# An attention and FFN kernel on one Trainium2 core: its build-time scheduler replaced by written-down tables of order, slots and engines

## The chip, the cores and the metric

The kernel runs on one NeuronCore of one Trainium2 chip. A core has five engines that each run their own stream of instructions in order: PE (TensorE, matrix multiplication), DVE (VectorE), ACT (ScalarE), POOL (GpSimd) and SP (SyncE, which here only issues DMA transfers). Matmuls write to PSUM; everything else lives in SBUF. The engines wait for each other by semaphores. The metric is the time of one execution on the device in microseconds, lower is better.

## The reference

Two parts follow each other. The first is causal attention over 4 batches, 8 heads, 768 tokens and head size 64, in which each query looks only at 6 chunks of 32 keys. Which ones is decided by an upper bound of the score, from the least and the greatest key of each chunk. The second is an FFN with a gate on the 3072 tokens.

```python
k_min, k_max = min and max of k over chunks of 32 tokens
ub = sum(maximum(q * k_min, q * k_max), axis=-1)       # 24 chunks for each query
ub = where(causal, ub, -1e9); top_chunks = argsort(ub)[..., -6:]
scores = q @ k.T / sqrt(64), masked to the top chunks and to earlier tokens
x = softmax(scores) @ v                                # 3072 tokens x 512
xn = x / sqrt(mean(x * x) + 1e-6) * rms_g
out = (silu(xn @ w_gate) * (xn @ w_val)) @ w_out       # 512 -> 1536 -> 512
```

Inputs and outputs are float32; matmuls of scores, values and FFN run in bf16, those of the upper bound in float32.

## The kernel before

**Tiling.** The tokens are cut into twelve blocks of 256 tokens: batch b, position m (0 to 2). They are handled in the order of a list at L501: (0,0), (1,0), (2,0), (3,0), (0,1), (1,1), (0,2), (2,1), (1,2), (3,1), (2,2), (3,2); "block 4" is the fifth of them, (0,1). Within a block the heads form two groups of four, 0 and 1.

**Attention of a block.** SP loads k, q and v (ACT helps for block 0). DVE transposes k and q in squares of 32 (L794) and takes the minimum and maximum of k for each chunk (L809). ACT or POOL converts them to bf16 ("half", L801 and L802). The upper bounds are float32 matmuls (`upper`, L680; L698 for the blocks with m = 0) of q, of its positive part ("relu", L888) and, for m > 0, of a copy with crossed partitions: SP copies these quarters from SBUF to SBUF by DMA ("qm", L864). DVE turns the bounds (L723), takes the greatest eight of each query (L739) and makes a mask (L745, L749, "swap" L755 or L759). Score matmuls (L922) add the mask by further small matmuls (L933); ACT exponentiates (L972); POOL clears the triangle of the diagonal (L942); value matmuls follow (L998); DVE divides by the sum (L1013, L1017).

**FFN of a block.** ACT squares and sums (L1034), POOL forms the inverse root (L1040, L1042). For blocks 0 to 3 DVE or ACT scales (L1066, L1068), PE transposes (L1078) and ACT or DVE evicts (L1087, L1091). For the later blocks DVE scales (L1052) and SP issues a transposing DMA ("across", L1058). Then come the gate and value matmuls (L1122): an FFN *piece* is eight matmuls of 256 columns, or sixteen of 128 in the half-block pieces of blocks 0 and 1. ACT takes the tanh (L1129), DVE multiplies (L1133), ACT copies the value half and POOL multiplies (L1141, L1144), or DVE does it directly (L1137). The projection (L1169) sums twelve matmuls of 512 columns, ten first and two later ("project" and "project+"); ACT or DVE evicts (L1184, L1187) and SP stores (L1191).

**Weights.** POOL issues nine loads of a third each of w_gate, w_val and w_out (`load_w` L625, `load_wo` L630), chained so that they stay in the order wg0, wv0, wg1, wv1, wg2, wv2, wo0, wo1, wo2. The first k, q and v loads of blocks 2 and 3 and the load of the norm's weights are tied to the landing of some of them (L584).

**What sets the order.** The program is not written in the order in which it runs. The code first makes a list of 1580 operations (`Plan.op`, L231): name, engine, a duration in which the engine is taken and one until the result is there, a function that emits the instructions, what it reads and writes, and which buffers of which pool it takes. Some (`flex`, L540) have two or three engines to choose from. Pools are small: four PSUM banks F for the upper bounds, transposes, values, FFN pieces and projections; two score buffers S, of which a score pass takes both; two output buffers; two to eighteen of the others (L453 to L480). `Plan.run` (L255) is a list scheduler at build time: it walks a modelled time forward, and for each engine picks, among the operations that could start, the one with the earliest due time of a table (`DUE`, L125). [...] It chooses the engine, hands out the buffer slots, and where PE would be idle before 60 us puts in filler matmuls ("warm", L1245) that write to a free bank. The emitted order is then fixed: on the chip each engine runs its stream in that order, and an operation that waits holds up everything behind it on its engine.

Of the kernel before, what the change touches and what calls it, by code (L numbers as in the profile page):

```python
# [11 lines left out]
ACT = mybir.ActivationFunctionType  # L12
# [7 lines left out]


# [15 lines left out]
class Rings:  # L37
    FETCHED = 3.3

    def __init__(self):  # L40
        self.now = 0.0
        self.queue = {}
        self.wait = []

    def _step(self, until):
        while True:
            heads = [q[0] for q in self.queue.values() if q]
            nxt = self.wait[0][0] if self.wait else None
            if not heads:
                if nxt is None or nxt > until:  # L50
                    return
                self.now = max(self.now, nxt)
            else:
                cycle = sum(d[1] for d in heads)
                end = self.now + min(d[0] for d in heads) * cycle
                stop = min(end, until, nxt if nxt is not None else end)
                if stop > self.now:
                    for d in heads:
                        d[0] -= (stop - self.now) / cycle
                    self.now = stop  # L60
                for q in self.queue.values():
                    if q and q[0][0] <= 1e-9:
                        q[0][2](self.now)
                        q.pop(0)
            while self.wait and self.wait[0][0] <= self.now + 1e-12:
                _, ring, d = self.wait.pop(0)
                ahead = sum(x[0] * x[1] for x in self.queue.get("POOL", ()))
                if ring != "POOL" and not d[3] and ahead > 0.0 and not self.queue.get(ring):
                    d[3] = True
                    self.wait.append((self.now + min(self.FETCHED, ahead), ring, d))  # L70
                    self.wait.sort(key=lambda w: w[0])
                    continue
                self.queue.setdefault(ring, []).append(d)
            if self.now >= until and not (self.wait and self.wait[0][0] <= until):
                if not any(q and q[0][0] <= 1e-9 for q in self.queue.values()):
                    return

    def add(self, t, ring, packets, cost, op):
        self._step(min(t, self.wait[0][0]) if self.wait else t)

        def landed(now, op=op):
            op.done = now + (0.9 if op.dma[2] else 1.2) + op.slack
        op.done = None
        self.wait.append((t, ring, [packets, cost, landed, False]))
        self.wait.sort(key=lambda w: w[0])
        self.guess()

    def room(self, ring, t):

        other = Rings()  # L90
        other.now = self.now
        other.queue = {r: [list(d) for d in q] for r, q in self.queue.items()}
        other.wait = [(w, r, list(d)) for w, r, d in self.wait]
        for q in list(other.queue.values()) + [[d for w, r, d in other.wait]]:
            for d in q:
                d[2] = lambda now: None

        def held():
            return sum(d[0] for d in other.queue.get(ring, ())) + sum(
                d[0] for w, r, d in other.wait if r == ring)  # L100

        while held() > 85.0:
            t = max(t, other.now) + 0.25
            other._step(t)
        return t

    def guess(self):
        other = Rings()
        other.now = self.now
        other.queue = {r: [list(d) for d in q] for r, q in self.queue.items()}  # L110
        other.wait = [(t, r, list(d)) for t, r, d in self.wait]
        other._step(1e9)


class Plan:

    SHARES = ("qx", "scale", "relu", "bd0", "bd1", "dk", "mk")
    PATIENT = {"DVE": 0.6, "ACT": 0.6}  # L120
    STICK = 25
    RESERVED = ("hh",)
    HOP = {"PE": 0.055, "ACT": 0.04, "DVE": 0.04, "POOL": 0.075, "SP": 0.06}

    DUE = (  # L125
# [129 lines left out]
    def run(self, in_order=(), fill=None):  # L255
# [4 lines left out]
        last = {}  # L260
# [1018 lines left out]
```

## Time and profile before

| | |
|---|---|
| median of 3 runs | 299.87 us (299.29 to 300.12) |
| profiled execution, from its first to its last instruction | 297.4 us |
| PE busy | 282.5 us (95%) |
| DVE, ACT, POOL busy | 217.1, 216.7, 155.6 us |
| DMA | 35.08 MB, 118 GB/s on the mean |
| mean granted TensorE clock | 0.997 |

Of the profiled execution the profile gives the span, not a time of its own as the runs have it; the median of the runs is 2.5 us above the span. In the profile's rows "L1122" is a line of the kernel; "F<-xsT,wg" says which tile is written from which; "x16" is a count of instructions. The page's chain of waits starts at the last instruction and goes back, at each step, to what released it. Matmuls are pipelined: a row's length includes the way through the array, so that the distance from one start to the next is the cost to PE.

### The profile page before, as it was taken

What the parts mean: (1) busy time and instruction counts of PE and PEld (TensorE: products, weight loads), DVE (VectorE), ACT (ScalarE), POOL (GpSimd) and SP (SyncE); (2) the same over time, 40 slices, a digit from 0 to 9 for tenths busy, and PEclk for the clock granted to TensorE, in tenths of its full rate; (3) what the DMA queues carried; (4) which work ended last, traced back from release to release, by engine and by line L of the source; (5) the groups of instructions that cost most, each with busy time, mean ns of one, the idle gap of its engine ahead of it and who ended that gap; (6) DMA issues with size and microseconds to landing.
All of it is one profiled execution on the core that took longest, in us unless ns stands there. A gap on an engine that the chain in (4) does not pass through costs nothing.

```text
span 297.4 us, 11418 instructions
## 1 busy us (share of the span) xinstructions
PE 282.5 (95%) x4672; PEld 213.4 (72%) x4672; DVE 217.1 (73%) x623; ACT 216.7 (73%) x372; POOL 155.6 (52%) x266
## 2 busy tenths in 40 slices
PE   7879999999999996999999999899999999999994
PEld 7548777657858854878767787488688778678763
DVE  6987774977998998888999999679356454456430
ACT  4897877688979876987985797677587668565331
POOL 4885858755976864475583276538044114214120
PEclk9999999999999999999999999999999999999998
DMA  7999998755676656654768576511014021011011
GB/s 188 208 204 206 255 197 163 159 130 134 141 194 154 144 136 103 149 100 110 205 135 162 108 193 150 133 40 39 0 57 55 1 82 30 2 73 35 2 71 71
DMA packets 86388, 35.08 MB, mean 118 GB/s; under 512 B 74816, under 2 KB 81728, under 8 KB 86336
## 3 DMA queue, kind: packets, MB, share of 16 engines
q1 hardware_dynamic: 80736, 29.12, 42.6%
q0 software_dynamic: 4752, 4.72, 9.4%
q8 instruction: 36, 0.59, 0.8%
q10 hardware_dynamic: 848, 0.53, 0.7%
q14 instruction: 16, 0.13, 0.2%
HBM read 28.58 MB, written 6.29 MB: 117 GB/s over the span
## 4 chain that ended last, share of the span: by engine, by line
PE 76%; DMA 9%; DVE 4%; ACT 4%; SPq 3%; POOL 1%; issue 1%; DVEq 0%; POOLq 0%; ACTq 0%
PE F L1122 39%; PE F L1169 18%; PE S L922 6%; PE F L998 6%; PE F L680 3%; SPq L528 3%; PE S L933 2%; DMA xsT<-xs 2%; DMA qraw<-in_q_dram 2%; DMA vraw<-in_v_dram 2%; DMA kraw<-in_k_dram 2%; DVE kx L809 1%; POOL hh L1144 1%; DVE m L739 1%; ACT th L1129 1%
## 5 line engine op out<-in xcount | busy, mean ns | idle before, releaser
L972 ACT ACTIVATE pt<-S 128x1024 bf16<-128x1024 f32 (+3 forms) x104 | 85.6, 857 | 19.7 <-PE S L933 18.2
L1144 POOL TENSOR_TENSOR hh<-tg,vs 128x512 bf16<-128x512 bf16 x48 | 55.7, 1164 | 42.6 <-ACT vs L1141 22.9
L1133 DVE SCALAR_TENSOR_TENSOR tg<-th,F 128x512 bf16<-128x512 bf16 x72 | 48.4, 680 | 39.3 <-ACT th L1129 33.7
L1122 PE MATMUL F<-xsT,wg 128*128 128x256 bf16 (+1 forms) x608 | 72.6, 267 | 3.7 <-DVE xnat L1017 1.7
L1122 PE MATMUL F<-xsT,wv 128*128 128x256 bf16 (+1 forms) x608 | 72.4, 267 | 0.6 <-DMA xsT<-xs 0.3
L1169 PE MATMUL F<-wo,hh 128*128 128x512 bf16 (+1 forms) x300 | 68.5, 371 | 1.8 <-POOL hh L1144 0.6
L1122 PEld LDWEIGHTS <-wg 128*128 128x128 bf16 x608 | 55.6, 98 | 13.5 <-issue 2.7
L1122 PEld LDWEIGHTS <-wv 128*128 128x128 bf16 x608 | 55.2, 98 | 9.7 <-DMA vraw<-in_v_dram 0.8
L1129 ACT ACTIVATE th<-F 128x512 bf16<-128x512 f32 x72 | 42.5, 598 | 19.7 <-PE F L1122 17.4
L942 POOL TENSOR_SCALAR_AFFINE_SELECT pt<-pt 128x512 bf16<-128x512 bf16 x48 | 32.2, 674 | 32.3 <-ACT pt L972 31.7
L1169 PEld LDWEIGHTS <-hh 128*128 128x128 bf16 x300 | 27.7, 98 | 28.4 <-issue 1.8
L1141 ACT ACTIVATE vs<-F 128x512 bf16<-128x512 f32 x48 | 28.7, 598 | 13.2 <-PE F L1122 10.1
L922 PE MATMUL S<-qb,kb 32*128 32x256 bf16 (+1 forms) x800 | 32.8, 253 | 2.3 <-ACT qb L801 2.0
L809 DVE TENSOR_REDUCE kx<-kT 128x16 f32<-128x512 f32 x48 | 30.4, 664 | 0.0
L998 PEld LDWEIGHTS <-pt 128*128 128x128 bf16 x672 | 24.8, 98 | 3.1 <-issue 0.3
L998 PE MATMUL F<-VX,pt 128*128 128x65 bf16 x672 | 26.6, 194 | 0.2 <-ACT vs L1141 0.2
L922 PEld LDWEIGHTS <-kb 32*128 32x128 bf16 x800 | 13.9, 92 | 15.0 <-issue 14.4
L933 PE MATMUL S<-mtd,chunkrow 32*128 32x128 bf16 (+2 forms) x384 | 20.5, 203 | 0.2 <-issue 0.2
L933 PE MATMUL S<-mto,chunkrow 32*128 32x128 bf16 (+2 forms) x384 | 19.9, 203 | 0.0
L1017 DVE TENSOR_TENSOR xnat<-F,rden 128x256 bf16<-128x256 f32 x48 | 19.2, 415 | 0.7
L933 PEld LDWEIGHTS <-chunkrow 32*128 32x128 bf16 x768 | 18.5, 93 | 1.2 <-issue 0.4
L1034 ACT ACTIVATE junk<-xnat 128x512 bf16<-128x512 bf16 x24 | 15.1, 631 | 5.4 <-DVE xnat L1017 5.0
(71 smaller groups left out, 337.2 us busy)
## 6 DMA issues: line engine op xcount, KB each, us to landing
vraw<-in_v_dram SPq DMA_DIRECT2D x24, 256.0 KB, 4.4
out_dram<-osb SPq DMA_DIRECT2D x23, 256.0 KB, 2.4
kraw<-in_k_dram SPq DMA_DIRECT2D x72, 64.0 KB, 2.4
qraw<-in_q_dram SPq DMA_DIRECT2D x72, 64.0 KB, 2.2
QX<-qT SPq DMA_DIRECT2D x32, 64.0 KB, 2.7
wg<-in_moe_w_gate_dram POOLq DMA_DIRECT2D x3, 512.0 KB, 12.3
wv<-in_moe_w_val_dram POOLq DMA_DIRECT2D x3, 512.0 KB, 14.3
wo<-in_moe_w_out_dram POOLq DMA_DIRECT2D x3, 512.0 KB, 23.5
```

The source lines that it names most:

```text
L809: plan.op(f"ext{n}{J}", "DVE", 0.585, 0.67, lambda n=n, op=op: VE.tensor_reduce(out=at(kx)[:, g, n], in_=at(kT).rearrange("p h (j c x) -> ...
L922: TE.matmul(s[a // 2][:, a % 2, c0:c0 + q1 - q0], kbt[r, t, ks], qbt[r, t, q0:q1], start=(t == 0), stop=(t == 1 and not mask), skip_group_ ...
L933: TE.matmul(o, chunkrow[r, BLK * kg + P * e:BLK * kg + P * (e + 1)], mv, start=False, stop=(d == 1), skip_group_check=True)
L942: GE.affine_select(out=d, in_=d, compare_op=ALU.is_ge, fill=0.0, base=0, pattern=[[0, 4], [1, P]], channel_multiplier=-1)
L972: lambda pt=pt, hs=hs, c0=c0, c1=c1, x=sc[hp]: SE.activation(out=at(pt)[:, hs, c0:c1], in_=at(x)[:, :, c0:c1], func=ACT.Exp, scale=SCALE), ...
L998: TE.matmul(o[:, a, :], p_[:, a, off:off + P], vt[:, e, a, :], start=(kb_ == 0 and a == 0), stop=(kb_ == nkb - 1 and a == 3), skip_group_c ...
L1122: TE.matmul(at(p_)[:, n * W:(n + 1) * W], w[:, g, ht * P:(ht + 1) * P], at(xT)[:, g, x0:x0 + W], start=(g == 0), stop=(g == NP - 1), skip_ ...
L1129: plan.op(f"tanh{U}.{hp}", "ACT", 0.48, 0.6, lambda th=th, gp=gp: SE.activation(out=at(th), in_=at(gp), func=ACT.Tanh, scale=0.5), pri - 0 ...
L1133: VE.scalar_tensor_tensor(out=at(tg), in0=at(th), scalar=1.0, in1=at(gp), op0=ALU.add, op1=ALU.mult), pri - 30, reads=[th, gp], writes=[tg ...
L1141: plan.op(f"vcopy{U}.{hp}", "ACT", 0.48, 0.6, lambda vs=vs, vp=vp: SE.activation(out=at(vs), in_=at(vp), func=ACT.Copy), pri + 0.1, reads= ...
L1144: plan.op(f"hh{U}.{hp}", "POOL", 1.11, 1.16, lambda tg=tg, vs=vs, hh=hh: GE.tensor_tensor(out=at(hh), in0=at(tg), in1=at(vs), op=ALU.mult) ...
L1169: TE.matmul(at(op)[:, cs], at(key)[:, o:o + P], wo[:, ht, cs], start=(ht == 0), stop=(ht == NHT - 1), skip_group_check=True)
```

## The change

The scheduler (`Rings`, `DUE`, the search in `Plan.run`) is removed. Four tables take its place: `SEQUENCE`, the numbers of all 1580 operations in one order, from which each engine's own order follows; `SLOTS`, the slot of each of the 1032 buffers; `CHOICE`, a letter (A, D or G for ACT, DVE or POOL) for each of the 206 operations with several engines; and `WARM`, nine places for filler with their counts. `run` only walks through the tables and asserts that an operation stands behind what it needs and that its slot is free. Some duration figures in the operations are edited too (the first blocks' conversions from 0.54 to 1.0, the mask row from 0.8 to 2.2, the weight loads' rate); nothing reads them any more. What each operation emits is unchanged.

```diff
-class Rings:
...
-    DUE = (
...
+SEQUENCE = [
+    22, 34, 37, 13, 33, 3, 35, 36, 14, 6, 38, 41, 18, 19, 4, 31, 24, 17, 29, 0, 7, 26, 39, 40, 1, 44, 48, 55,
...
+    1574, 1571, 1575, 1577, 1578, 1579]
+SLOTS = [
...
+CHOICE = (
+    "GGGGAADGGAGAAGAADDDDAGGGGADDGAGDGGAADADDGDGDGAGDDGGDGGDGDAAGGDGGAGGDGDGDGGADAGGAAGGGGGDAGGADGGGDGGGG"
+    "AAGGDGGADGDGGAAGGGGGGGGGGGAGGAGGGGDAAGGAGGGGGGAGAAGDDGGGGGGAGGGDGAGGGDAGGGGAGGAGAAAAAAAAADAAADAADDAA"
+    "ADDADA")
+WARM = [
+    (58, 86, 0, 0), (72, 4, 2, 1), (97, 10, 0, 1), (140, 6, 2, 1), (166, 2, 3, 1), (174, 5, 2, 1), (183, 1, 1,
+    1), (267, 1, 3, 1), (339, 1, 0, 1)]
...
-    def run(self, in_order=(), fill=None):
+    def run(self, fill):
+        keys = list(self.pool_of)
         left = {k: len(v) for k, v in self.readers.items()}
+        self.slot = dict(zip(keys, SLOTS))
...
+        engine = dict(zip((o.seq for o in self.ops if len(o.alts) > 1), CHOICE))
...
+        for place, x in enumerate(SEQUENCE):
+            for n, slot, wide in warm.get(place, ()):
...
+            o = self.ops[x]
+            assert all(d.seq in gone for d in o.deps + o.after) and x not in gone
+            if x in engine:
+                o.eng = self.NAMES[engine[x]]
+            o.occ, o.lat, o.fn = o.alts[o.eng]
             for key in o.takes:
...
+                place_ = (self.pool_of[key], self.slot[key])
+                assert held[place_] is None, (o.name, place_, held[place_])
+                held[place_] = key
```

The numbers say little by themselves, so here is what the tables hold, read against the list of operations. PE keeps 315 operations, and on the mean one stands 2.9 places from where it stood. ACT has 314 (before 330), DVE 436 (426), POOL 253 (247), SP 262 (262). A change of matmul shape from one PE operation to the next occurs 116 times (121). Filler is 86 narrow and 30 wide matmuls (77 and 39).

PE's order from the first FFN piece to block 1's first piece ("wg0(0) h0" is the gate piece of block 0's first half, "wg0 h6" that of the whole block from hidden tile 6; s, v, t are score pass, values, transpose with block and head group or half; "fill n" is n wide fillers):

```
before: wg0(0) h0, s1.1a, wv0(0) h0, t0.1, s1.0b, fill 2, wg0(1) h0, wg0 h4, s1.1b, wg0 h6, wv0(1) h0, wv0 h6,
        v1.0, v1.1, v1.0, v1.1, wv0 h4, fill 6, wg0 h8, wg0 h10, t1.0, fill 3, t1.1, wg1(0) h0
after:  wg0(0) h0, wv0(0) h0, fill 2, v1.0, s1.1a, fill 5, t0.1, s1.0b, fill 1, wg0 h6, v1.1, wg0(1) h0, wv0 h4,
        wv0(1) h0, s1.1b, wg0 h4, v1.0, wv0 h6, wg0 h10, v1.1, t1.0, wg0 h8, wg1(0) h0
```

The first loads on SP, and the weight loads' places on POOL (among its 253 or 247 operations):

```
SP before: k0 k0 q0 q0 v0 v0 k1 k1 k1 k1 q1 q1 q1 q1 v1 v1        POOL before: wg0 35, wv0 36, wg1 38, wv1 40, wg2 41, wv2 42, wo0 44, wo1 53, wo2 54
SP after:  k0 k0 q0 q0 k1 q1 k1 q1 q1 k1 q1 k1 v0 v0 v1 v1        POOL after:  wg0 34, wv0 42, wg1 46, wv1 49, wg2 55, wv2 56, wo0 59, wo1 61, wo2 75
```

POOL's constants (the memsets of "ones", BO and BD), all done before block 0's work in the old order, are partly spread between that work in the new one: before wg0 there now stand a conversion of block 0's k, block 0's two positive parts and four products for the bounds, and of block 1 one positive part and one q conversion.

More of the change, by code (lines that the diff above doesn't have):

```diff
@@ L34, in __init__ @@
         self.alts = {eng: (occ, lat, fn)}
-class Rings:
[L38 to L112, printed above, removed]
@@ L115 @@
-class Plan:
[L119 to L123, printed above, removed]
-    DUE = (
[91 rows of a table removed]
-    )
+class Plan:
+    NAMES = {"P": "PE", "A": "ACT", "D": "DVE", "G": "POOL", "S": "SP"}
     def __init__(self):
@@ L392, in run @@
             for key in o.uses:
-                last[key] = max(last.get(key, 0.0), o.done)
                 left[key] -= 1
                 if not left[key]:
-                    self.free[self.pool_of[key]].append((last[key], slot[key]))
+                    held[self.pool_of[key], self.slot[key]] = None
+            gone.add(x)
             order.append(o)
-            for u in o.users:
-                n_dep[u.seq] -= 1
-                if not n_dep[u.seq]:
-                    offer(u)
         self.order = order
-        self.span = max(o.done for o in order)
@@ L565, in constants @@
             -378, reads=["ident"], writes=["pat"])
-        plan.op("chunkrow", "DVE", 0.8, 0.9, lambda: VE.tensor_scalar(
+        plan.op("chunkrow", "DVE", 2.2, 2.28, lambda: VE.tensor_scalar(
             out=chunkrow.rearrange("p (c t) -> p c t", t=CH),
@@ L1245, in keep_busy @@
             TE.matmul(store["F"][slot][:, 0:x.shape[1]], ident[:], x, start=True, stop=True)
-    for o in plan.run(in_order=("kraw", "qraw", "vraw", "kT", "qT", "kb", "qb", "QX", "VX", "xsT", "xs", "hh", "xnat"),
-                      fill=(1.6, 5.6, 60.0, 0.0565, 0.216, "F", keep_busy)):
+    for o in plan.run(("F", keep_busy)):
         o.fn()
```

169 lines of the change are left out of this document (27 added, 142 removed), and 197 rows, old and new, of tables (DUE, SEQUENCE, SLOTS).

## The prediction

> **What bounds the kernel now.** I read the head of the page and its chain of waits first, then the engines' busy time in stretches, cut at the first FFN matmul (22.8 us) and at the last long wait of the start (38.6 us).
>
> ```profile
> span 297.4 us, 11418 instructions
> ...
> PE 76%; DMA 9%; DVE 4%; ACT 4%; SPq 3%; POOL 1%; issue 1%; DVEq 0%; POOLq 0%; ACTq 0%
> ...
> core 0: us, PE busy (x) PEld busy (x) DVE busy (x) ACT busy (x) POOL busy (x), PEclk, DMA share, GB/s
> 0.00:22.80 22.80, 18.35 (x349) 13.33 (x349) 18.30 (x55) 17.46 (x33) 16.84 (x60) 1.00 1.03 200
> 22.80:38.60 15.80, 14.71 (x238) 11.70 (x234) 12.07 (x33) 13.52 (x32) 11.57 (x20) 1.00 1.19 228
> 38.60:60.00 21.40, 21.31 (x324) 16.37 (x326) 15.18 (x46) 15.13 (x28) 15.00 (x25) 1.00 0.89 171
> 60.00:100.00 40.00, 38.77 (x636) 28.96 (x636) 35.39 (x120) 35.36 (x67) 27.08 (x40) 1.00 0.62 152
> 100.00:140.00 40.00, 36.67 (x723) 28.34 (x721) 34.57 (x112) 31.57 (x53) 25.14 (x37) 1.00 0.57 121
> 140.00:180.00 40.00, 40.00 (x759) 30.20 (x761) 38.23 (x115) 33.05 (x54) 20.49 (x37) 1.00 0.70 158
> 180.00:220.00 40.00, 39.13 (x718) 28.86 (x707) 27.20 (x85) 27.68 (x44) 18.53 (x28) 1.00 0.27 68
> 220.00:260.00 40.00, 40.00 (x667) 30.31 (x666) 20.23 (x37) 28.77 (x43) 13.19 (x16) 1.00 0.16 35
> 260.00:297.40 37.40, 33.56 (x291) 25.38 (x289) 15.89 (x27) 14.17 (x26) 7.76 (x8) 0.98 0.15 50
> ```
>
> PE is the bound: its work is 76% of the chain, and from 38.6 us on it is hardly ever empty. An order can only win what PE loses. Length less PE busy is 4.45 us before 22.8, 1.09 up to 38.6, 0.09 up to 60, then 1.23, 3.33, 0, 0.87, 0 and 3.84. The last 3.84 is nearly all the end (last matmuls, eviction, store), whose order stays almost as it was. Beside idle time there is filler, matmuls that only keep PE running, all before 38 us:
>
> ```profile
> L1245 PE MATMUL F<-chunkrow,ident 128*128 128x512 bf16 x39 | 10.2, 380 | 0.0
> L1245 PE MATMUL F<-ident 128*128 128x128 bf16 x77 | 6.4, 265 | 1.7 <-POOL eps L551 1.7
> ```
>
> The DMA engines are full there (share 1.03 and 1.19), so the start is paced by what arrives, and by how fast DVE and ACT turn it into the first FFN operand.
>
> **The change part by part.** Every operation is still issued once; only order, slots and engine choices differ. The durations edited in the code fed the planner that is deleted, and cost nothing on the chip.
>
> *Start, to the first FFN piece.* SP now issues block 1's k and q ahead of block 0's v. DVE does block 1's q transposes and min/max ahead of block 0's first normalisations. The first scale and the first transposed eviction go from ACT to DVE.
>
> ```profile
> 7.27 1.31 DVE L794 STREAM_TRANSPOSE qT<-qraw 128x512 f32<-128x512 f32 x2 [0.33 <-DMA qraw<-in_q_dram]
> 8.49 1.83 DVE L809 TENSOR_REDUCE kx<-kT 128x16 f32<-128x512 f32 x3
> 15.44 0.42 DVE L1017 TENSOR_TENSOR xnat<-F,rden 128x256 bf16<-128x256 f32 x1
> ...
> 19.19 0.73 ACT L1068 ACTIVATE xs<-xnat,ri_all 128x512 bf16<-128x512 bf16 x1
> 21.06 1.15 ACT L1087 ACTIVATE xsT<-F,rmsg 128x128 bf16<-128x128 bf16 x4
> ...
> 22.85 1.07 PE L1122 MATMUL F<-xsT,wg 128*128 128x128 bf16 x16
> 38.65 1.05 PE L1122 MATMUL F<-xsT,wg 128*128 128x128 bf16 x16 [0.73 <-ACT xsT L1087]
> ...
> L1091 DVE TENSOR_TENSOR xsT<-F,rmsg 128x512 bf16<-128x512 bf16 x2 | 1.4, 692 | 0.3 <-PE F L1078 0.2
> L1066 DVE TENSOR_SCALAR xs<-xnat,ri_all 128x512 bf16<-128x512 bf16 x2 | 0.7, 350 | 0.1
> ```
>
> Ahead of the normalisation that ended at 15.86 us DVE now has two more transposes (0.65 each) and four more reduces (0.61 each), 3.7 us. DVE is idle for 4.50 of the first 22.8 us (22.80 less 18.30), 1.69 of that before its first instruction, so up to 2.8 us can go into gaps. The normalisation ends between 15.86 + 0.9 = 16.8 and 15.86 + 3.7 = 19.6; I take 17.9, nearer the packed end, since q of block 1 no longer arrives behind v. From it to the first FFN matmul took 22.85 - 15.86 = 7.0 us. On DVE the scale is 0.38 shorter (0.73 to 0.35) and the eviction 0.46 (1.15 to 0.69), and both leave the ACT queue, where the scale began 3.3 us after the normalisation's end and the eviction 1.1 us after the scale. I estimate 3.9 us for what is left (square, mean, scale, transpose, eviction, with their hops). First FFN piece: 21.8, between 20.7 and 23.5.
>
> *First FFN piece to 38.65.* I laid the two PE orders side by side from the tables. Between the first piece and block 1's first piece both hold the same ten FFN pieces, three score passes and four value products; the new one has 8 instead of 11 wide fillers and one transpose less. A wide filler is 0.216 us (the chain row of 512-wide matmuls below, 2.16 for 10), a transpose of four about as much. So 15.80 becomes 14.9 with its 1.09 us of idle kept, 13.8 without; 14.35 is the middle. Block 1's first piece comes at 21.8 + 14.35 = 36.15, 2.5 earlier; the moved transpose gives 0.1 back. **Start: -2.4**, between -4.0 and +0.6.
>
> *Weights behind it.* POOL used to issue all weight loads early; now each stands behind named work. The first stands behind block 1's q conversion, the last, a third of w_out, behind a product of block 0's FFN.
>
> ```profile
> 9.80 0.99 POOL L528 DMA_DIRECT2D wg<-in_moe_w_gate_dram  x1
> 20.90 1.61 POOL L528 DMA_DIRECT2D wo<-in_moe_w_out_dram  x2
> ...
> 41.30 1.16 POOL L1144 TENSOR_TENSOR hh<-tg,vs 128x512 bf16<-128x512 bf16 x1 [0.53 <-ACT vs L1141]
> ...
> DMA to landing us min/median/max: 22.6/23.5/25.2
> DMA to landing us min/median/max: 7.9/17.8/25.2
> ...
> 49.72 2.16 PE F L1169 x10
> ```
>
> The first landing row is of the w_out loads alone, the second of all nine weight loads. The early issue bought queueing: a w_out load took 22.6 to 25.2 us, the last one, issued about 21.7, landing near 47. The bytes ahead of it are the same in both orders, so with full engines it should land as before; the first projection, which needs all of w_out, started at 49.7. It can therefore move up by the 2.4 us of the start, to just about the landing. I cost the move at nothing; without that cover each microsecond of lateness is one of PE.
>
> *Waits after 38.6 us.* The largest lie in one place:
>
> ```profile
> 105.37 3.54 SPq L528 DMA_DIRECT2D qraw<-in_q_dram  x6
> 108.96 1.87 SPq L864 DMA_DIRECT2D QX<-qT  x3
> 112.08 2.62 SPq L1058 DMA_TRANSPOSE xsT<-xs  x2
> ...
> 107.14 2.42 DVE L809 TENSOR_REDUCE kx<-kT 128x16 f32<-128x512 f32 x4
> ...
> 110.84 1.04 PE L1169 MATMUL F<-wo,hh 128*128 128x512 bf16 x4
> 111.81 0.94 PE L680 MATMUL F<-QX,BD 64*32 64x128 f32 x16
> 113.20 0.48 PE L680 MATMUL F<-qraw,BD 64*32 64x128 f32 x10 [0.44 <-POOL qraw L888]
> 117.58 1.05 PE L1122 MATMUL F<-xsT,wg 128*128 128x256 bf16 x8 [1.72 <-DVE xnat L1017]
> ```
>
> The upper bounds (L680) wait for copies that SP issues behind q loads at 0.6 us each. In the new table the last copy is 6 places earlier on SP (about 3.5 us), and PE reaches the bounds only 0.86 us sooner (four projection matmuls later instead of earlier): the 0.44 goes. The FFN of block 4 waits 1.72 us for transposed rows. Their chain loses two of the four reduces ahead of the scale (1.2 us), gains one gate product (estimated at a reduce's 0.6) and is 3 places earlier on SP; cover on PE is the same ten operations. I take half, 0.86. Of the other 3.27 us between 60 and 220 (5.43 less 2.16), whose places are all re-ordered, a third: 1.1. In block 5 one FFN piece and one score pass less stand ahead of the same wait (estimated from the 0.9 us of a projection's four matmuls as some 1.6 us less cover), against two operations that leave the DVE path ahead of the scale (about 1.2, as two reduces): +0.4, taken as +0.5. **Waits: -1.9**, between -5.4 (all gone) and +4.
>
> *Switches.* Going between full, row-tiled and quadrant matmuls leaves 0.97 - 4 x 0.216 = 0.11 us (110.84 to 111.81). The tables have 116 such changes on PE, before 121: **-0.5**.
>
> *Engine choices.* ACT has 314 operations in the tables, before 330; POOL 253, before 247; DVE 436, before 426.
>
> ```profile
> L802 POOL CAST qb<-qT 128x512 bf16<-128x512 f32 x16 | 10.6, 659 | 4.5 <-PE S L922 2.6 <-DVE qT L794 1.4 <-DVE rden L1013 0.5
> ```
>
> At such a conversion's length that is some 10 us off ACT, and, as small operations leave POOL for larger ones, an estimated 14 onto it. POOL's busy column adds up to 155.6 of 297.4, and DVE has idle time everywhere but in 140 to 180 us (1.77): hidden, and a rival if not.
>
> Sum: -2.4 - 1.9 - 0.5 = -4.8. The profiled span is 297.4, the median of the runs 299.87, 2.5 above, which start and end around the span add. 299.87 - 4.8 = **295.1 us**.
>
> [...] The shorter filler leaves PE gaps in the first 21.8 us: filler falls from 28 wide and 77 narrow to 20 and 86, and I expect up to 2 us of idle in one piece.
>
> ```profile
> 4.00:6.00 2.00, 2.00 (x24) 2.00 (x22) 1.46 (x4) 0.37 (x2) 0.29 (x2) 1.00 0.87 253
> 6.00:8.00 2.00, 2.00 (x38) 1.92 (x35) 1.67 (x4) 1.91 (x2) 0.00 (x0) 1.00 1.16 221
> ```
>
> In the filler alone PE did 24 matmuls in 2 us at first, then 38: it starts at about 0.6 of its later rate, whatever the clock column says. [...]
>
> **The rivals.**
> 1. *Nearly all PE waits go* and the start reaches its early bound: -4.0 - 4.8 - 0.5, 290.6. For it: every engine has idle time beside PE. Against: four banks and two score buffers still tie PE to ACT and DVE. 0.19.
> 2. *The weights come late* (the slower side): w_out's last load is issued behind a product of block 0's FFN that ran at 41.3 us. With the shortest landing of the rows (7.9) it lands at 49, with the shortest of a w_out load (22.6) at 64. At 54, 13 us after its issue, the first projection starts 4.3 late and the start's gain is gone: 299.87 + 4.3 - 1.9 - 0.5 = 301.8. It decides at a landing of 52.1, where lateness eats the other two gains. For it: the load stands at place 75 on POOL, before at 54. Against: with full DMA engines the bytes, not the issue, set the landing. 0.15.
> 3. *DVE absorbs it*: at 38.23 of 40 busy in 140 to 180 us it can't follow a PE that is 3 us ahead, and the waits come back there: only the switches remain, 299.4. Against: DVE has 16.3 us idle between 38.6 and 140 (6.22 + 4.61 + 5.43) that it could use. 0.06.
> 4. *The clock falls in the start*: 4 us of FFN pieces at 24/38 of the rate cost 1.5: 296.6. 0.03.
> 5. *The start gives nothing*, since arrivals pace it: 299.87 - 2.4 = 297.5. 0.10.
>
> **How the numbers follow.** My forecast has 0.47; alone it spans 292.5 to 297.0. 0.3%, 0.9 us, is about what runs of this kernel (299.29 to 300.12) can tell from no change. Faster: 0.47 + 0.19 + 0.10 + 0.03 = 0.79; same 0.05 and slower 0.16 from rivals 2 and 3 (0.01 of rival 3 falls on the slower side). The range runs from 289.5, just below rival 1, to 301.0, which leaves out the worse half of rival 2.
>
> **What the new profile would show.** Right: the first FFN matmul at 20.7 to 23.5 us, block 1's first piece near 36; first projection near 47, with no wait for w_out; L680 without the 0.44 us wait; about 9 us of PE idle beside start and end filler cut to 30 wide ones; ACT about 10 us less busy, POOL about 14 more. Wrong: PE waiting on a weight load or on POOL before 55 us, or DVE at its limit with PE idle between 140 and 180 us.

## The result, and the profile after

The tables made the kernel slower: 307.76 us, median of 4 runs (307.13 to 309.81), against 299.90 (299.29 to 300.12) for the kernel before on the same chip. The ratio is 1.0254, 95% interval 1.0203 to 1.0305. The forecast was 295.1, its range ended at 301.0. (Here and below, ratios and intervals leave out runs more than 1.5% above the fastest of the same kernel, four of eleven in the run with the wait for scale10 alone and at most two elsewhere; medians and spreads are of all runs.) The profiled execution of the new kernel took 307.62 us, 305.9 of them from its first to its last instruction.

The head of its page, the busy times and the chain that ended last:

```profile
span 305.9 us, 11386 instructions
...
PE 285.5 (93%) x4672; PEld 217.5 (71%) x4672; DVE 226.8 (74%) x633; ACT 204.3 (67%) x353; POOL 162.5 (53%) x272
...
PE 52%; DVE 18%; DMA 12%; SPq 6%; POOL 4%; issue 4%; ACT 2%; ACTq 0%; DVEq 0%; POOLq 0%
```

PE's share of the chain fell from 76% to 52%, DVE's rose from 4% to 18%. Of the 8.5 us that the span grew (305.9 less 297.4), PE is idle for 5.5 (20.4 against 14.9, span less busy) and busy for 3.0 longer (285.5 against 282.5) although nine wide fillers became narrow ones. The stretches of the prediction's table (columns as there) say where:

```profile
0.00:22.80 22.80, 18.86 (x373) 14.93 (x374) 16.69 (x57) 14.07 (x26) 15.62 (x57) 1.00 0.95 205
22.80:38.60 15.80, 13.30 (x204) 10.45 (x202) 13.34 (x29) 11.11 (x27) 11.85 (x17) 0.93 1.12 214
38.60:60.00 21.40, 18.71 (x276) 15.05 (x274) 19.50 (x41) 12.37 (x21) 14.49 (x20) 0.89 0.82 159
...
100.00:140.00 40.00, 36.53 (x770) 28.74 (x769) 35.02 (x124) 31.99 (x53) 28.27 (x42) 1.00 0.64 134
...
180.00:220.00 40.00, 36.90 (x711) 28.75 (x710) 30.56 (x95) 27.84 (x44) 18.60 (x27) 0.96 0.34 77
```

PE idle went from 1.09 to 2.50 us in the second stretch, from 0.09 to 2.69 in the third and from 0.87 to 3.10 in 180 to 220; in 100 to 140 it is 3.47, before 3.33. In the same three stretches, and only there, the granted clock (the column after POOL) is below its value of before, which made PE's own work longer (in two profiles further down the same six fillers take 2.67 us at 0.50 and 1.47 at 1.00). PE's order of time shows one long wait in each place:

```profile
34.61 1.05 PE L949 MATMUL F<-xsT,wg 128*128 128x256 bf16 x8 [1.78 <-DMA wg<-in_moe_w_gate_dram]
...
53.69 1.54 PE L949 MATMUL F<-xsT,wv 128*128 128x128 bf16 x13 [2.44 <-DVE tg L960]
...
189.88 1.17 PE L825 MATMUL F<-VX,pt 128*128 128x65 bf16 x20 [3.02 <-DVE tg L960]
```

and finer windows of PE alone (busy, count, granted clock, DMA share, GB/s), two for each gap, show the clock behind it:

```profile
33.04:36.45 3.41, 1.15 (x12) 1.00 1.22 226
36.45:39.86 3.41, 3.41 (x30) 0.50 1.24 207
50.11:53.52 3.41, 1.15 (x13) 1.00 1.22 214
53.52:56.93 3.41, 3.24 (x51) 0.50 0.61 120
186.64:190.05 3.41, 0.40 (x9) 1.00 0.39 61
190.05:193.46 3.41, 3.41 (x55) 0.50 0.61 133
```

Each time the granted clock is 0.50 for 3.41 us, which costs up to 1.7 us of full-rate work (an estimate: half of 3.41), 5.1 us for the three. Not every such gap has this behind it, as the last section shows.

What does DVE do ahead of its late tg (DVE's product with the tanh, which frees PE's bank)? In order of time, around 33 us and 48 us, first DVE, then POOL, whose hh is the product of gate and value half and whose pt is the triangle of the diagonal (each row begins with its start and its length):

```profile
32.88 3.00 DVE L893 TENSOR_SCALAR xs<-xnat,ri_all 128x512 bf16<-128x512 bf16 x1
...
48.37 4.67 DVE L572 TENSOR_TENSOR mk<-ubn,m 128x64 bf16<-128x64 f32 x1
52.96 0.67 DVE L960 SCALAR_TENSOR_TENSOR tg<-th,F 128x512 bf16<-128x512 bf16 x1
...
32.84 0.65 POOL L769 TENSOR_SCALAR_AFFINE_SELECT pt<-pt 128x512 bf16<-128x512 bf16 x1
33.45 2.27 POOL L971 TENSOR_TENSOR hh<-tg,vs 128x512 bf16<-128x512 bf16 x2
...
47.85 3.38 POOL L971 TENSOR_TENSOR hh<-tg,vs 128x512 bf16<-128x512 bf16 x3
51.18 0.63 POOL L769 TENSOR_SCALAR_AFFINE_SELECT pt<-pt 128x512 bf16<-128x512 bf16 x1
51.78 0.60 POOL L731 CAST VX<-vraw 128x512 bf16<-128x512 f32 x1
52.34 0.62 POOL L769 TENSOR_SCALAR_AFFINE_SELECT pt<-pt 128x512 bf16<-128x512 bf16 x1
```

The scale of block 1's first half ("scale10") took 3.00 us, against 0.35 for the same shape before; the mask of block (2,0), head group 1 ("mk(2,0,1)") took 4.67, where before no mask of any of the three shapes took longer than 0.99:

```profile
L745 DVE TENSOR_TENSOR mk<-ubn,m x15: 204/651/987, 12.2 to 206.7; 128x512 bf16<-128x512 f32 x8, 128x64 bf16<-128x64 f32 x6, 128x128 bf16<-128x128 f32 x1
```

Both began while POOL worked without a break and ended when POOL had nothing to do: at 35.88 behind the hh that ended at 35.72, at 53.04 behind the triangle that ended at 52.96. The planner that the change removes had a rule against just this (in its modelled time it never let an operation of a list of names, "scale" and "mk" among them, start on DVE while a POOL operation of over 0.15 us ran); tables hold an order, not a distance in time.

One operation outside that list had shown the same in the profile before: the row of chunk masks, written at the start, took 2.28 us beside POOL's memsets, and 0.55 in the changed kernel, where those memsets are spread:

```profile
2.17 2.28 DVE L566 TENSOR_SCALAR chunkrow<-pat 128x768 bf16<-128x768 bf16 x1
```

The third place is another kind. DVE's order of time there:

```profile
183.13 0.74 DVE L879 SCALAR_TENSOR_TENSOR xs<-xnat,ri_all,gB 128x512 bf16<-128x512 bf16 x1
186.96 1.24 DVE L715 TENSOR_SCALAR qraw<-QX 128x512 f32<-128x512 f32 x1 [3.09 <-DMA QX<-qT]
188.12 0.99 DVE L466 TENSOR_REDUCE BD<-kx 128x64 f32<-128x64 f32 x5
189.14 0.69 DVE L960 SCALAR_TENSOR_TENSOR tg<-th,F 128x512 bf16<-128x512 bf16 x1
```

The relu of block (2,2), group 0, is on DVE now and waits 3.09 us for SP's copies; the tg behind it, whose tanh was done at 185.19, frees the PSUM bank for PE's value product and comes at 189.14.

### The profile page after: what moved, and what is told of

The parts are those of the page before. It is cut to its first block, busy times and chain, and to the rows that moved or that the text cites. A ratio compares the mean times of both kernels' runs of the same rounds, so it can differ in the third digit from the quotient of the medians.

```text
span 305.9 us, 11386 instructions
## 1 busy us (share of the span) xinstructions
PE 285.5 (93%) x4672; PEld 217.5 (71%) x4672; DVE 226.8 (74%) x633; ACT 204.3 (67%) x353; POOL 162.5 (53%) x272
## 4 chain that ended last, share of the span: by engine, by line
PE 52%; DVE 18%; DMA 12%; SPq 6%; POOL 4%; issue 4%; ACT 2%; ACTq 0%; DVEq 0%; POOLq 0%
PE F L949 25%; PE F L996 14%; PE S L749 5%; PE F L825 5%; SPq L354 4%; DMA kraw<-in_k_dram 4%; DVE kx L636 3%; DMA QX<-qT 2%; DMA wg<-in_moe_w_gate_dram 2%; DMA qraw<-in_q_dram 2%; DVE kT L621 2%; PE S L760 2%; DVE tg L960 2%; DVE xs L879 2%; DVE m L566 2%
## 5 line engine op out<-in xcount | busy, mean ns | idle before, releaser
L949 PE MATMUL F<-xsT,wg 128*128 128x256 bf16 (+1 forms) x608 | 73.4, 270 | 3.4 <-DMA wg<-in_moe_w_gate_dram 1.8
L949 PE MATMUL F<-xsT,wv 128*128 128x256 bf16 (+1 forms) x608 | 73.6, 270 | 2.5 <-DVE tg L960 2.4
L960 DVE SCALAR_TENSOR_TENSOR tg<-th,F 128x512 bf16<-128x512 bf16 x72 | 48.5, 678 | 27.8 <-ACT th L956 24.3
L949 PEld LDWEIGHTS <-wv 128*128 128x128 bf16 x608 | 56.3, 99 | 11.6 <-issue 2.8
L769 POOL TENSOR_SCALAR_AFFINE_SELECT pt<-pt 128x512 bf16<-128x512 bf16 x48 | 31.3, 658 | 28.8 <-ACT pt L799 28.6
L825 PE MATMUL F<-VX,pt 128*128 128x65 bf16 x672 | 28.8, 195 | 7.2 <-DVE tg L960 3.0
L825 PEld LDWEIGHTS <-pt 128*128 128x128 bf16 x672 | 26.7, 99 | 11.1 <-issue 6.7
L749 PE MATMUL S<-qb,kb 32*128 32x256 bf16 (+1 forms) x800 | 33.6, 258 | 0.1
L964 DVE TENSOR_TENSOR hh<-tg,F 128x512 bf16<-128x512 bf16 x24 | 16.2, 677 | 12.6 <-PE F L949 12.1
L844 DVE TENSOR_TENSOR xnat<-F,rden 128x256 bf16<-128x256 f32 x48 | 19.9, 419 | 1.0
```

The costliest lines, as they stand in the source:

```text
L749: TE.matmul(s[a // 2][:, a % 2, c0:c0 + q1 - q0], kbt[r, t, ks], qbt[r, t, q0:q1], start=(t == 0), stop=(t == 1 and not mask), skip_group_ ...
L769: GE.affine_select(out=d, in_=d, compare_op=ALU.is_ge, fill=0.0, base=0, pattern=[[0, 4], [1, P]], channel_multiplier=-1)
L825: TE.matmul(o[:, a, :], p_[:, a, off:off + P], vt[:, e, a, :], start=(kb_ == 0 and a == 0), stop=(kb_ == nkb - 1 and a == 3), skip_group_c ...
L949: TE.matmul(at(p_)[:, n * W:(n + 1) * W], w[:, g, ht * P:(ht + 1) * P], at(xT)[:, g, x0:x0 + W], start=(g == 0), stop=(g == NP - 1), skip_ ...
L960: VE.scalar_tensor_tensor(out=at(tg), in0=at(th), scalar=1.0, in1=at(gp), op0=ALU.add, op1=ALU.mult), pri - 30, reads=[th, gp], writes=[tg ...
```

## The experiments

My theory after the comparison: two DVE operations stand still beside a busy POOL (A1, at 33 and 48 us), one DVE operation waits for a copy at the head of its queue (A2, at 184 us), and the clock falls behind each gap. The main rival: the weights come late (wg2 landed at 34.56, before 32.08; wo2 at 54.48, before 47.00), and the DVE stalls hide in their shadow. All variants are the changed kernel with two small lists applied to its tables:

```diff
+MOVES = []    # (operation, the operation that it is put ahead of in SEQUENCE)
+HOLDS = []    # (operation, an operation that it waits for)
...
+        for n, y in MOVES:
+            todo.remove(seq[n])
+            todo.insert(todo.index(seq[y]), seq[n])
...
+        if o.name in holds:
+            tc.add_manual_dep(o.inst.ins, named[holds[o.name]].inst.ins.name, ...)
```

so that their line numbers are 13 higher (L893 is L906, L572 is L585, L960 is L973), and 17 higher in the run with the choices undone.

### Two waits on POOL

```diff
-HOLDS = []
+HOLDS = [('hh(0, (1,)).0', 'scale10'), ('hh(1, (0, 1)).4', 'mk(2, 0, 1)')]
```

> Two waits are added on POOL and nothing else is changed: hh of block 0's piece (1,) 0 waits for scale10, and hh of block 1's piece 4 waits for mk(2,0,1), so that each of these two DVE operations finds POOL idle once. Theory A (a DVE operation stands still while POOL works without a break): scale10 falls from 3.00 to under 1 us, mk(2,0,1) from 4.67 to under 1 us, the 2.44 us idle of PE before the value projection of block 1's second token half goes, and the time is 302.5 to 305. Rival B (the late weights hold the kernel there): the two operations may become short, but PE then stands as long for wg2 (landed 34.56) and wo2 (landed 54.48), and the time is 306.5 to 308.5. Rival C (the two operations are long for another reason): they stay at 3.0 and 4.7 us, and the time is 307 to 310.

Ratio to before 1.0052 (1.0020 to 1.0084), median 302.1: about 6.0 us of the 7.6 came back (ratios times 300), a little more than theory A expected. The two DVE operations, and POOL's wait behind the second:

```profile
34.21 1.14 DVE L906 TENSOR_SCALAR xs<-xnat,ri_all 128x512 bf16<-128x512 bf16 x1
...
48.41 0.75 DVE L585 TENSOR_TENSOR mk<-ubn,m 128x64 bf16<-128x64 f32 x1
...
49.30 2.27 POOL L984 TENSOR_TENSOR hh<-tg,vs 128x512 bf16<-128x512 bf16 x2 [0.24 <-DVE mk L585]
```

One wait of 0.24 us on POOL turned 4.67 us on DVE into 0.75: the mask ended at 49.16, right behind the one POOL operation that ran when it began (a product, 47.89 to 49.06). PE's 2.44 us wait is gone. Rival C is out: the two operations are long because of POOL. The scale fell to 1.14, a little above "under 1". Each wait was then tried alone.

```diff
-HOLDS = []
+HOLDS = [('hh(1, (0, 1)).4', 'mk(2, 0, 1)')]
```

> The changed kernel with one added wait: hh of block 1's piece 4 waits for mk(2,0,1). Theory (the stall at 48 us is worth what PE lost there, +4.2 us between 20 and 30 us of its work): 303 to 305. Rival (PE reaches wo2's landing at 54.5 first, so that only 2 to 3 of it come back): 305 to 306.

```diff
-HOLDS = []
+HOLDS = [('hh(0, (1,)).0', 'scale10')]
```

> The changed kernel with the other wait alone: hh of block 0's piece (1,) 0 waits for scale10. Theory (worth 1 to 2 us by itself, since wg2's landing at 34.6 is right ahead of it): 305.5 to 307. Rival (the slack behind it takes it up, nothing comes back): 307 to 308.5.

With the wait for mk alone the ratio is 1.0111 (1.0065 to 1.0157), median 303.7: inside the theory's 303 to 305. The scale still took 3.36 us there, at 33.51. With the wait for scale10 alone it is 1.0081 (1.0042 to 1.0120), better than either expectation, and with the widest spread (300.6 to 308.1); its profile still has the mask at full length:

```profile
47.94 4.69 DVE L585 TENSOR_TENSOR mk<-ubn,m 128x64 bf16<-128x64 f32 x1
```

By the ratios the two alone are worth 4.3 and 5.2 us, by the medians 4.1 and 3.5, and both together 6.0 or 5.6: the prices don't add. The clock may have a part in this: in the last profile PE still waits 2.45 us behind the mask, up to 53.28, and the clock stays at 1.00 there. In the same profile the relu near 184 us also cost PE 1.3 us instead of 3.0, with nothing changed there, so a part of its gain is a later wait that came out shorter.

### One DVE operation moved

```diff
-MOVES = []
+MOVES = [('relu(2, 2, 0)', 'turn k(3, 2, 0)')]    # behind KX(2,2) and tg of piece 8
```

> One DVE operation is moved: relu(2,2,0) goes behind KX(2,2) and tg of block 6's piece 8, so that DVE no longer waits 3.09 us at it for the QX copies while both are ready. Theory A: the 3.02 us idle of PE before values(1,2,0)0 and the low clock behind it go, and the time is 303.5 to 305.5. Rival B (PE has slack there, because the copies, vx(3,1,1) or project6.1 hold it at once): 306.5 to 308.5.

Ratio 1.0181 (1.0149 to 1.0212), median 305.4: 2.2 us back, at the upper edge of what I expected, because the next wait stood behind:

```profile
187.54 1.09 DVE L728 TENSOR_SCALAR qraw<-QX 128x512 f32<-128x512 f32 x1 [0.58 <-DMA QX<-qT]
...
190.20 0.69 DVE L973 SCALAR_TENSOR_TENSOR tg<-th,F 128x512 bf16<-128x512 bf16 x1
...
190.94 1.24 PE L1009 MATMUL F<-wo,hh 128*128 128x512 bf16 x5 [1.60 <-DVE tg L973]
```

The relu still waits and still runs beside POOL (1.09 us; the relu that began in a gap of POOL at 85.61 in the changed kernel's profile took 0.41), and now the projection waits 1.60 us for the tg behind it.

### Both

```diff
-MOVES = []
-HOLDS = []
+MOVES = [('relu(2, 2, 0)', 'turn k(3, 2, 0)')]
+HOLDS = [('hh(0, (1,)).0', 'scale10'), ('hh(1, (0, 1)).4', 'mk(2, 0, 1)')]
```

> The two added POOL waits and the moved relu together. Theory A: the gains are at different times and add up, 298 to 301.5, that is, the time of the kernel before again. Rival: the later gain is taken back by what the earlier one triggers, 303 to 306.

Ratio 0.9999 (0.9967 to 1.0031), median 300.8: the time of the kernel before, as the theory had it. Two waits and one move take back the whole loss, and no more. In its profile (span 296.6) the relu takes its 0.42:

```profile
180.83 0.42 DVE L728 TENSOR_SCALAR qraw<-QX 128x512 f32<-128x512 f32 x1
```

### The rival: weights earlier

```diff
-MOVES = []
+MOVES = [('wg2', 'tri(1, 0, 0)a'), ('wv2', 'tri(1, 0, 0)a'), ('wo0', 'tri(1, 0, 1)a'),
+         ('wo1', 'hh(0, (0,)).0'), ('wo2', 'hh(0, (0,)).0')]
```

> The last five weight transfers are issued earlier, in gaps of POOL of the changed kernel: wg2 and wv2 at about 22 instead of 26.1 and 26.9, wo0 at about 25, wo1 and wo2 at about 26 and 27 instead of 32.0 and 47.0. Theory A: what stood behind the late weights is the DVE operations, so wg2's 1.78 us idle is taken over by scale10 and nothing changes at mk(2,0,1): 306 to 308.5. Rival B (the late weights hold the kernel): 302.5 to 305.

Ratio 1.0145 (1.0077 to 1.0214), median 305.3: 3.3 us back, between the two expectations. But the profile has the two DVE operations short without any added wait, and block 2's keys late:

```profile
34.63 0.71 DVE L634 STREAM_TRANSPOSE kT<-kraw 128x512 f32<-128x512 f32 x1 [2.11 <-DMA kraw<-in_k_dram]
...
37.26 0.69 DVE L906 TENSOR_SCALAR xs<-xnat,ri_all 128x512 bf16<-128x512 bf16 x1
...
50.20 0.75 DVE L585 TENSOR_TENSOR mk<-ubn,m 128x64 bf16<-128x64 f32 x1
```

The loads shifted everything in time, and both operations came out short (0.69 and 0.75 us) without the waits. So this run doesn't price the weights. A run further down, which moves only wg2 and wv2, does it in a kernel without the stalls.

### The engine choices without the order, and the order without the choices

```diff
-        engine = dict(zip((o.seq for o in self.ops if len(o.alts) > 1), CHOICE))
+        engine = dict(zip((o.seq for o in self.ops if len(o.alts) > 1), BEFORE))   # 85 letters differ
```

> The changed kernel's order, buffer slots and PE fills, but all 85 operations that the change put on another engine are back on the engine that they had before (each at its new place in the order). Theory A (the choices cost, because they put work on DVE and POOL that then stands in each other's way, and on DVE behind a copy): scale10 on ACT and relu(2,2,0) on POOL take away two of the three stalls, 301 to 305. Rival (the choices are free, as the prediction had it, and the order alone costs): 306 to 309.

Ratio 1.0282 (1.0248 to 1.0317), median 309.3: my theory that the choices cost was wrong here, the rival's 306 to 309 (just exceeded) was right. With scale10 back on ACT, DVE stands still at two other operations, one of which has only 16 elements in each partition:

```profile
37.32 2.95 DVE L659 TENSOR_TENSOR kx<-kx 128x16 f32<-128x16 f32 x1
...
50.22 2.96 DVE L589 TENSOR_TENSOR mk<-ubn,m 128x64 bf16<-128x64 f32 x1
```

So it is not one certain operation that loses the time: with other engines chosen, other DVE operations stood for 2.95 and 2.96 us near the same places.

```diff
-SEQUENCE = [22, 34, 37, ...]
+SEQUENCE = [24, 12, 34, ...]    # the order, slots and fills of the kernel before; CHOICE stays the new one
```

> The other half: the order, slots and fills of the kernel before, written as tables, with the changed kernel's 85 engine choices. Theory A (the choices cost by themselves): 302 to 307, with at least one DVE operation of over 2 us. Rival (free choices): 299.5 to 301.

Ratio 1.0153 (1.0112 to 1.0195), median 304.9. The time is what the theory had, the mechanism is not: no DVE operation took 2 us or more but the mask row at the start (2.29, before 2.28). Instead an operation that moves to another engine moves into another queue, and small waits sum up all along, as in these two stretches, in which PE idles 2.72 and 1.22 us (before 1.23 and 0):

```profile
60.00:100.00 40.00, 37.28 (x573) 27.20 (x571) 35.01 (x108) 28.94 (x56) 28.91 (x43) 1.00 0.58 141
...
140.00:180.00 40.00, 38.78 (x717) 29.25 (x715) 36.65 (x116) 29.59 (x50) 20.91 (x36) 1.00 0.66 160
```

So neither half is free and neither half is the cause by itself; order and choices fit each other, and each is bad with the other's partner.

### Is the predicted gain behind the stalls?

The kernel with both mended is as fast as before, not 4.8 us faster. A first candidate was the clock in the start. PE's window from 19 to 21 us (clock after the count) in the changed kernel, then in the kernel with both mended:

```profile
19.00:21.00 2.00, 1.78 (x18) 1.00 1.25 205
```
```profile
19.00:21.00 2.00, 2.00 (x13) 0.50 1.22 200
```

Of the eight profiles that have the changed kernel's start and fills with its engine choices, two show 1.00 there and six 0.50. At 0.50 the six fillers ahead of the first FFN transpose take 2.67 us instead of 1.47, and the first FFN piece comes at 23.03 instead of 21.55; in the kernel before it came at 22.85.

```profile
19.09 2.67 PE L1085 MATMUL F<-chunkrow,ident 128*128 128x512 bf16 x6
```

```diff
-        for at, n, slot, wide in WARM:
+        for at, n, slot, wide in WARM + [(103, 3, 3, 1), (124, 5, 3, 1)]:
```

> The kernel with both added POOL waits and the moved relu, and with eight more filling matrix multiplications on PE, three before values(0,0,1)0 and five before values(0,0,0)1, where PE waits 1.0 and 1.4 us at 14 to 17 us. Theory: the granted clock stood at 0.50 from 19 to 21 in that kernel (1.00 in the changed one's profile), which stretched the six filling multiplications before the first turn from 1.3 to 2.5 us; with the fills the clock stays at 1.00 and the time falls by 1 to 2, to 298 to 300. Rival (the clock there hangs on something else, or the start is not on the path): 300 to 302.

Ratio 1.0036 (1.0005 to 1.0067), median 301.3: nothing gained. The clock did hold, 1.00 in all these windows, and the first FFN piece came at 22.41 instead of 23.03; but the five fillers stood behind a wait for the norm whose bank they wrote to, and held the values up themselves, from 17.28 to 18.30:

```profile
17.23 1.24 PE L1085 MATMUL F<-chunkrow,ident 128*128 128x512 bf16 x5 [0.95 <-DVE xnat L857]
18.30 0.42 PE L838 MATMUL F<-VX,pt 128*128 128x65 bf16 x8
```

So with more fill the clock stood at 1.00 in this profile, but the time did not fall with it.

```diff
-MOVES = [('relu(2, 2, 0)', 'turn k(3, 2, 0)')]
+MOVES = [('relu(2, 2, 0)', 'turn k(3, 2, 0)'), ('across40', 'store1.1'), ('load q1231', 'store1.1'),
+         ('across41', 'store2.1'), ('tri(1, 1, 1)0', 'dk(2, 1, 1)')]
```

> The same with four places of the order changed: the two transposes of block 4 are issued ahead of a load of queries and two stores on SP (they are ready at 108.9 and 109.9 and go out at 110.8 and 112.3, wg of block 4 waits 1.7 us for them), and tri(1,1,1)0 goes ahead of a POOL operation, half q and relu that wait for a copy (values(1,1,1)1 waits 1.6 us for it). Theory (waits of an order can be taken out one at a time once nothing triggers a new one): 2 to 3 less than without the moves, 295 to 298. Rival (the next wait takes their place): 298 to 300.

Ratio 1.0018 (0.9987 to 1.0050), median 300.8. The rival was nearer. The moves did win at their own place (PE's waits of 1.21 and 1.69 us near 117 and 123 became 1.05 and less than 0.2), but block 5 now waits 1.50 us at 133, and the same relu waited again for copies, ran beside POOL, and PE's wait behind it grew from 1.60 to 2.50:

```profile
182.81 1.22 DVE L728 TENSOR_SCALAR qraw<-QX 128x512 f32<-128x512 f32 x1 [1.35 <-DMA QX<-qT]
```
```profile
186.33 2.32 PE L1009 MATMUL F<-wo,hh 128*128 128x512 bf16 x10 [2.50 <-DVE tg L973]
```

```diff
-MOVES = [('relu(2, 2, 0)', 'turn k(3, 2, 0)'), ...
+MOVES = [('relu(2, 2, 0)', 'turn k(3, 2, 1)'), ...
-        for at, n, slot, wide in WARM + [(103, 3, 3, 1), (124, 5, 3, 1)]:
+        for at, n, slot, wide in WARM + [(103, 3, 3, 1), (109, 3, 3, 1)]:
```

> The kernel with four places changed, and relu(2,2,0) moved once more on DVE, behind the swap, tg and hh of block 6's piece 10 instead of ahead of them; the five filling multiplications before values(0,0,0)1, which waited for a norm, are replaced by three before values(0,0,0)0. Theory A (DVE's order around relu is what costs 2.7 us there: relu waits for the QX copies till 182.7, takes 1.22 us while POOL works, and tg of piece 10, whose F bank project6.1 needs, ends only at 186.3): project6.1 starts right behind scores(1,2,1)0 and the time is 296.5 to 299. Rival (the copies or POOL's hh hold project6.1 all the same): 299.5 to 301.5.

Ratio 1.0027 (1.0001 to 1.0053), median 301.8: the rival's time or just above it. The projection's 2.50 us wait is gone, as expected, but 50 us earlier block 5's wait for its transposing DMA grew from 1.50 to 2.13:

```profile
135.17 1.03 PE L962 MATMUL F<-xsT,wg 128*128 128x256 bf16 x8 [2.13 <-DMA xsT<-xs]
```

```diff
-MOVES = [...]
+MOVES = [..., ('wg2', 'tri(1, 0, 0)a'), ('wv2', 'tri(1, 0, 0)a')]
```

> The same, with wg2 and wv2 issued at about 22 instead of 26. Theory A (the late weights cost little): the wait of 1.0 to 1.5 us for wg2 near 35 goes and the next wait, for values(1,0,1)1 or block 1's xsT, takes 0.5 to 1 of it back; 0.3 to 1 less than without. Rival B (weights had been the bound of the start): 2 or more less. Rival C (the earlier transfers take DMA time from the loads of queries and keys): the same or up to 1 more.

Ratio 1.0099 (1.0062 to 1.0136), median 303.2, 2.2 us more than without (0.0072 of 300): the sign is rival C's, the size larger than it gave. PE's wait for wg2 (0.84 us) is gone, and a longer one has taken its place, since block 2's keys take 5.0 to 6.9 us to land, without the move 3.0 to 3.2, and block 1's norm stands behind them on DVE. DVE, then PE:

```profile
35.15 0.71 DVE L634 STREAM_TRANSPOSE kT<-kraw 128x512 f32<-128x512 f32 x1 [3.28 <-DMA kraw<-in_k_dram]
```
```profile
38.56 0.42 PE L838 MATMUL F<-VX,pt 128*128 128x65 bf16 x8 [2.96 <-DVE xnat L857]
```

This answers the rival for w_gate and w_val: earlier loads cost more than they bring. Earlier w_out loads were not tried in a kernel without the stalls.

The last one keeps SP's order and the fills of the changed kernel, and mends a third stall:

```diff
-MOVES = []
-HOLDS = []
+MOVES = [('relu(2, 2, 0)', 'turn k(3, 2, 1)'), ('tri(1, 1, 1)0', 'dk(2, 1, 1)')]
+HOLDS = [('hh(0, (1,)).0', 'scale10'), ('hh(1, (0, 1)).4', 'mk(2, 0, 1)'), ('hh(2, (0, 1)).8', 'scale31')]
```

> The changed kernel with three added POOL waits (for scale10, mk(2,0,1) and scale31), relu(2,2,0) behind the hh of block 6's piece 10, and tri(1,1,1)0 ahead of the POOL operations that wait for copies; no fills, and SP's order as in the changed kernel. Theory (each mended wait keeps its worth when no transfer is moved with it): 297 to 299, faster than both kernels. Rival (the kernel's other waits take it back): 299.5 to 301.5.

Ratio 0.9994 (0.9962 to 1.0026), median 300.5. The rival was right: the same time as before. PE is busy for 282.4 us of 297.5 there, before 282.5 of 297.4. None of these versions beats the kernel before.

## Why the prediction was wrong, step by step

**Start (-2.4): right at its first point, lost at its second.** The first FFN piece came at 21.55 (21.8 predicted), by the way that the sum took: the normalisation ended at 17.74 (17.9), and 3.8 us followed (3.9). Block 1's first piece came at 38.83 instead of 36.15: where I had put 14.35 us there were 17.28, with scale10 standing for 3.00 us, 1.78 us for wg2 and 3.41 us at half clock. And the first point itself holds only where the clock does, in two of eight profiles; in the others the piece came at 23.03 to 24.37. The term was worth nothing (38.83 against 38.65 before).

**Weights ("I cost the move at nothing").** "The bytes ahead of it are the same in both orders, so with full engines it should land as before" was false: wo2 landed at 54.48 instead of 47.00, wg2 2.5 us later. For w_out it cost nothing that shows, as PE reached its first projection only at 57.71. For wg2 it cost a 1.78 us wait, which the sum lacked; yet issuing it earlier made the kernel slower. Rival 2 (0.15) had the right side and nearly the right landing (it decided at 52.1), but not the cause: in the kernel with both mended the projections began at 51.98, with no wait for w_out, whose last third landed at about 52.1, again later than in the kernel before.

**Waits after 38.6 us (-1.9, between -5.4 and +4): the step that failed.** PE's idle time from 38.6 to 220 us grew by 4.6 us (2.69 + 0.80 + 3.47 + 0.06 + 3.10 = 10.12 against 5.52), and the half clock behind the gaps took more. The single waits that I followed through the queues came out in the right direction: the 0.44 us of L680 are gone, block 4's 1.72 became 1.3. What was wrong was the rest of the sum, "a third" of the waits whose places are re-ordered taken as a gain, from before's waits alone. A new order makes new waits where there were none, and the wait behind the mask was in 38.6 to 60, a stage that had 0.09 us to lose. Nor was the gain hidden behind the stalls: with both mended, PE's idle time from 38.6 to 220 us is 5.68 us (0.33 + 0.88 + 4.05 + 0.06 + 0.36), 0.2 more than before, where the sum had 1.9 less.

**The planner removed ("cost nothing on the chip").** The durations do cost nothing. But in its modelled time the planner had kept operations such as scale10 and the mask from starting beside a working POOL, and I never asked what happens when nothing does. That is the missing term: the two added waits alone give 6.0 us back.

**Engine choices (hidden, 0).** ACT is 12.4 us less busy (10 predicted), POOL 6.9 more (14 predicted); DVE, to which I gave ten operations more and no price, is 9.7 more busy, of which the two stalls are about 7. Not hidden: in the old order the choices cost 1.5%; in the new order their undoing brought nothing (1.0282 against 1.0254). Rival 3 placed DVE's limit in 140 to 180 us; there PE idled 0.06 us.

**Switches (-0.5).** Nothing in the profiles shows it apart from the rest.

**The clock (rival 4, 0.03).** My forecast had the clock hold across gaps of up to 2 us. It was at 0.50 for 3.41 us behind one of 1.78 with one of 0.69 behind it, behind 2.44 and behind 3.02, and in six of eight starts, where no gap since the first matmul was above 1.25. Rival 4 thus came about in most profiles of the start. Its price of 1.5 us was too low by its own working (pieces of 4 us at 24/38 of the rate take 6.3, 2.3 more); the first piece came 1.5 later at half clock (23.03 against 21.55), for six fillers and not for FFN pieces.

## What to carry to other kernels

A search that orders instructions by traced durations keeps the order and loses the distance in time on which it relied: where an operation of one engine stands still beside the work of another, as scale10 (3.00 us) and the mask (4.67) did here, keeping the two apart has to become an order on the chip (one wait of POOL for a DVE operation cost 0.24 us and saved 3.9 on DVE). Before costing a re-ordering, ask of each rule that the old order was made under what keeps it on the chip once the planner is gone; a row far above its usual length, such as the 2.28 us of the mask row, shows where to ask. And on a queue in order, put an operation that waits for a DMA behind what is ready, or its wait becomes that of everything behind it (the relu's 3.09 us on DVE were followed by 3.02 on PE).

## What the runs showed of the hardware

**DVE beside POOL.** In the changed kernel's profile a small DVE operation stood still not for one POOL operation but for several that followed without a gap: mk(2,0,1) for 4.67 us across six (three products, two triangles, a conversion), scale10 for 3.00 across three. These ended when POOL was idle, 0.08 and 0.16 us behind its last operation. It isn't always so: in the run with the moved relu, the relu (187.54, 1.09 us) was through at 188.63, in the middle of two products of POOL that followed each other directly:

```profile
187.20 2.46 POOL L984 TENSOR_TENSOR hh<-tg,vs 128x512 bf16<-128x512 bf16 x2
```

What lets one operation through between two of POOL and not another was not found. The operations named here that took over 2 us (scale10, masks, kx and the mask row) were TENSOR_SCALARs and TENSOR_TENSORs with their inputs in SBUF; the SCALAR_TENSOR_TENSOR tg, with one input in PSUM, took 0.69 us beside a working POOL (from 49.62 in the run with the two waits, beside products from 49.30 to 51.57). The longest of the POOL operations that mk(2,0,1) stood across took about 1.2 us, so its 4.67 were not a wait for one of them.

**The clock.** In the changed kernel's profile each of the three longest gaps (1.78, 2.44 and 3.02 us) was followed by 3.41 us at 0.50, from 36.45, 53.52 and 190.05; six of the eight thinly filled starts had as long or longer at 0.50, and in the profile with eight more fillers it was 1.00 there. The length of a gap does not settle it. Of 14 gaps of 2.0 to 3.1 us in all the profiles behind the start, seven were followed by this and seven were not, among them 2.96 us with wg2 earlier, 2.50 with four places moved and 2.29 with the two waits on POOL. In the 3.41 us ahead of the three dips of the changed kernel PE was busy for 1.15, 1.15 and 0.40 us. With four places moved the clock stayed at 1.00 over the gap of 2.50, which ended at 186.33, and behind it:

```profile
182.18:185.59 3.41, 1.65 (x55) 1.00 0.36 78
185.59:189.00 3.41, 2.67 (x42) 1.00 0.74 157
```

What sets which gap is followed by the lower clock was not shown.

**Spread.** The kernel before ran from 298.8 to 302.2 us over all its runs here; the mended tables spread from 298.2 to 303.8. One order has several times. The clock seems to have a share in that, though not the whole: with the wait for scale10 alone, runs of 300.6, 300.9 and 304.3 us had a mean clock of 1.000, those of 306.6 and 308.1 had 0.981 and 0.978.
